# A new load order and a newly searched instruction list for a pre-LN block with memory attention and a SiLU feed-forward

## The chip, the cores and the metric

The kernel runs on one core of a Trainium2 chip. The time is the device time of one execution, in microseconds (us). A core has five engines that run their own instruction streams and meet only at semaphores: TensorE (PE in the profile, its weight loads PEld), VectorE (DVE), ScalarE (ACT), GpSimd (POOL) and SyncE (SP). SP does nothing here but issue transfers; ACT issues some as well.

## The reference

x is 2048 tokens by 640, in bf16.

```python
h  = x + A(layernorm(x), wq, wk, wv, wo, beta)
h2 = h + silu(layernorm(h) @ w1) @ w2            # w1 640 x 1728, w2 1728 x 640
# A: 32 heads of 20, the tokens in 4 segments of 512, for each segment s:
a_dot = softmax(q k^T * scale + causal mask) @ v     # inside the segment
a_mem = (phi(q) @ M) / (phi(q) @ z + 1e-6)           # phi(t) = t + 1 if t > 0 else exp(t)
o     = g * a_mem + (1 - g) * a_dot                  # g = sigmoid(beta), per head
M    += phi(k)^T @ v ;  z += sum(phi(k))             # for the segments behind
# A returns o @ wo
```

## The kernel before, in words

Everything stays in the core's memories; each weight is loaded once. The tokens are worked on in blocks of 128 (16 blocks, four to a segment). For a block the layer norm is three tasks: `n1_st` (two BN_STATS and a BN_AGGR on DVE, lines 728 and 731), `n1_r` (the reciprocal root on POOL, lines 741 and 744, its first step on DVE line 738 where the list says so) and `n1_ap` (DVE, line 750, writes `xn_rot`). The first four blocks are transposed on PE against an identity (`n1_tp`, line 759) and copied to `hT` by ACT (`n1_te`, line 768); later blocks are transposed by a transfer that SP issues (`n1_tr`, line 774, into `xT`).

wq and wk come in raw (into memory that `sT` uses later) and are rearranged into `wqr` and `wkr`, so that the heads lie on 32-row strips: ten tasks `re_wq0` to `re_wk4`, of two or three copies each, on DVE (line 694) or ACT (line 692). Then PE forms q and k in five chunks c for each of the two weights w (`pr`, line 837; in segment 0 each in two halves x and y of 256 tokens, so 5 matmuls of 256 columns per task), and ACT (line 845) or DVE (line 846) copies them out (`qe`). In segment 0 q and k lie in memory that w2 takes later, so the profile calls them `w_sb`; from segment 1 on they are `QK`. Twelve small copies by DMA per segment (`vt`, line 877) put together the last three groups of heads; they are issued by SP or ACT. `v` (line 802) and its copies `ve` (ACT line 812, DVE line 813) give the values `Vx`.

The heads are worked on in eight groups g of four. Scores are `qk` on PE (line 914), the exponential `e` on ACT (line 925, into `PT`, two heads at a time), the causal mask `mk` on POOL (line 936), probabilities times values `av` on PE (line 957), its copy `oe` (ACT line 970, DVE line 972), `tn` and `nm` (lines 986, 990 and 1003 to 1031) transpose back, add the memory term and divide. phi is `ex` on ACT (line 852) and `pha`, `phb` on DVE (lines 859 and 865); the memory update is `kt` (a transposing transfer, line 1071), `mz`, `ma`, `mb` (line 1079 ff.). Then come the output projection (`ot`, a transposing transfer, line 1132, and `wo`, line 1140), the second layer norm (`n2_`), the feed-forward `h1` (line 1175; its last part line 1169), `th` and `s` (tanh on ACT line 1184, product on DVE line 1190), `h2` (line 1217), the sum `o` (DVE line 1230) and the store `out` (line 1235).

No planner runs when the kernel is built. The string ORDER lists all 1479 tasks; `Graph.schedule` (line 287) goes down the list, and each task adds its instructions at the end of its engine's stream. An entry is the task's name, after a slash the engine where the task may choose (A is ACT, D is DVE, G is POOL, S is SP; without it the first that the task allows), and behind the colon the numbers of the buffers that it takes. So the list sets, for every engine, the order of its instructions; the waits follow from which task reads or writes what. An engine that waits holds up all that is behind it in its stream. `fillN` stands for N matmuls of zeros (line 614), which nothing reads.

The first loads are issued by lines 576 and 579. Before the change SP issues x0 (block 0), wq, three fifths of wv, beta, x4 (blocks 4 to 7), wo and w1 with the last rows of w2; ACT issues x1, x2, x3, wk, the rest of wv and x8 (blocks 8 to 11). `warm` (line 595) is a tanh on ACT that brings in the table of functions.

## Time and profile before

| what | value |
|---|---|
| device time, three executions | 310.89, 307.36 and 311.02 us, median 310.89 |
| profiled execution: span from first to last instruction | 307.5 us |
| PE busy | 293.9 us, 96% of the span |
| ACT busy | 224.4 us, 73% |
| DVE busy | 221.8 us, 72% |
| POOL busy | 141.3 us, 46% |
| read from HBM, written | 10.41 MB, 2.62 MB |
| mean granted TensorE clock | 0.989 |

The profiled execution's own time is not listed apart from its span; the span of 307.5 us is close to the lowest of the three times. In the profile, the busy shares by slices show where an engine is full, the granted clock (PEclk) in tenths shows where TensorE ran below full speed, the timeline gives start and duration of merged runs of like instructions ("x10" is ten of them), and a note in square brackets gives the idle time ahead of a row and what ended it. The matmuls are pipelined, so a run of n of them takes less than n times the duration of one.

### The profile page before, as it was taken

How to read it: one execution, taken by the hardware profiler on the slowest of the kernel's cores; microseconds unless marked ns; L12 is line 12 of the kernel's file. 1: busy time of each engine (PE TensorE's matmuls, PEld its weight loads, DVE VectorE, ACT ScalarE, POOL GpSimd, SP SyncE). 2: the span in 40 equal slices, each digit the busy share in tenths (PEclk: the TensorE clock that was granted, in tenths of full speed). 3: DMA queues.
4: the chain of work that ended last, by engine and by line, in shares of the span. 5: the costliest groups of instructions: out<-in, count | busy, mean ns of one | idle time of the engine just before them, and what ended most of it. 6: DMA issues, size and time to landing. Idle time of an engine off the chain costs nothing.

```text
span 307.5 us, 7509 instructions
## 1 busy us (share of the span) xinstructions
PE 293.9 (96%) x3010; PEld 171.8 (56%) x3010; DVE 221.8 (72%) x513; ACT 224.4 (73%) x319; POOL 141.3 (46%) x271
## 2 busy tenths in 40 slices
PE   7699889999999999997999999999999999999996
PEld 5476545455555555655553554466664557764574
DVE  5679877879669498986689886857965686834533
ACT  3489998999999889996859899986679851004500
POOL 7569652424654746752655445663573530100000
PEclk9689999999999999999999999999999999999999
DMA  7993624405465310144153320224220004221001
GB/s 262 316 370 84 114 61 126 107 19 159 83 90 110 41 33 9 35 81 52 38 120 95 67 36 17 36 52 92 64 66 23 0 3 84 66 65 44 0 30 58
DMA packets 48738, 24.66 MB, mean 80 GB/s; under 512 B 39168, under 2 KB 47616, under 8 KB 48704
## 3 DMA queue, kind: packets, MB, share of 16 engines
q1 hardware_dynamic: 44884, 19.62, 28.4%
q10 hardware_dynamic: 3820, 4.56, 5.0%
q8 instruction: 24, 0.39, 0.5%
q14 instruction: 10, 0.08, 0.1%
HBM read 10.41 MB, written 2.62 MB: 42 GB/s over the span
## 4 chain that ended last, share of the span: by engine, by line
PE 74%; ACT 9%; DVE 7%; DMA 6%; issue 1%; ACTq 1%; SPq 1%; DVEq 0%
PE ps_all L1217 20%; PE ps_all L1175 15%; PE ps_all L837 11%; ACT PT L925 7%; PE ps_all L914 7%; PE ps_all L1140 6%; PE ps_all L957 5%; PE ps_all L802 5%; DMA sT<-in_A_wk_dram 3%; PE ps_all L986 2%; DMA oT<-otok 2%; PE ps_all L1079 1%; PE ps_all L990 1%; DMA w_sb<-w_sb 1%; DVE stt L728 1%; DVE oTs L972 1%
## 5 line engine op out<-in xcount | busy, mean ns | idle before, releaser
L925 ACT ACTIVATE PT<-ps_all 128x1024 bf16<-128x1024 f32 (+1 forms) x168 | 157.0, 986 | 14.4 <-PE ps_all L914 12.5
L936 POOL TENSOR_SCALAR_AFFINE_SELECT PT<-PT 128x512 bf16<-128x512 bf16 x128 | 82.6, 651 | 78.3 <-ACT PT L925 75.1
L1217 PE MATMUL ps_all<-w_sb,sT 128*128 128x320 bf16 (+2 forms) x462 | 65.1, 295 | 0.1
L1175 PE MATMUL ps_all<-hT,w_sb 128*128 128x512 bf16 (+1 forms) x325 | 63.2, 337 | 0.0
L1184 ACT ACTIVATE th<-ps_all 128x512 f32<-128x512 f32 (+2 forms) x70 | 34.6, 508 | 37.8 <-PE ps_all L1169 19.5
L1217 PEld LDWEIGHTS ps_all<-w_sb,sT 128*128 128x128 bf16 x462 | 43.6, 98 | 18.8 <-issue 1.8
L1190 DVE SCALAR_TENSOR_TENSOR sT<-th,ps_all 128x512 bf16<-128x512 f32 (+2 forms) x70 | 38.4, 562 | 20.0 <-ACT th L1184 19.4
L1175 PEld LDWEIGHTS ps_all<-hT,w_sb 128*128 128x128 bf16 x325 | 29.7, 98 | 24.4 <-issue 2.1
L728 DVE BATCH_NORM_STATS2 stt<-x_tok 128x6 f32<-128x320 bf16 x64 | 28.0, 479 | 2.8 <-DMA x_tok<-in_A_x_dram 2.4
L1230 DVE SCALAR_TENSOR_TENSOR x_tok<-ps_all,x_tok 128x640 bf16<-128x640 f32 (+3 forms) x18 | 13.3, 746 | 18.2 <-PE ps_all L1217 18.0
L1140 PE MATMUL ps_all<-wo_sb,oT 128*128 128x320 bf16 x160 | 24.4, 300 | 1.9 <-DMA oT<-otok 1.9
L1031 POOL TENSOR_TENSOR otok<-on 128x320 bf16<-128x320 bf16 x24 | 19.2, 800 | 15.2 <-DVE on L1023 15.2
L957 PE MATMUL ps_all<-PT,Vx 128*32 128x256 bf16 (+3 forms) x576 | 23.5, 287 | 1.2 <-DVE rd L1003 0.8
L744 POOL TENSOR_TENSOR rst<-rst,eps_c 128x1 f32<-128x1 f32 x32 | 18.5, 577 | 11.4 <-DVE rst L738 9.6
L846 DVE CAST QK<-ps_all 128x512 bf16<-128x512 f32 x25 | 17.2, 687 | 5.6 <-PE ps_all L837 5.3
L972 DVE TENSOR_SCALAR oTs<-ps_all,lsc 128x512 bf16<-128x512 f32 (+1 forms) x29 | 17.7, 617 | 4.8 <-PE ps_all L957 4.5
L1023 DVE TENSOR_TENSOR on<-ps_all,rd 128x640 bf16<-128x640 f32 x24 | 19.8, 824 | 0.8
L1140 PEld LDWEIGHTS ps_all<-wo_sb,oT 128*128 128x128 bf16 x160 | 14.7, 98 | 9.4 <-DMA oT<-otok 2.2
L750 DVE TENSOR_SCALAR xn_rot<-x_tok,mvt,rst 128x640 bf16<-128x640 bf16 x32 | 15.7, 498 | 5.2 <-POOL rst L744 5.2
L837 PE MATMUL ps_all<-xT,wqr 128*128 128x512 bf16 x75 | 18.7, 380 | 0.3 <-ACT PT L925 0.3
L837 PE MATMUL ps_all<-xT,wkr 128*128 128x512 bf16 x75 | 18.7, 380 | 0.1
L957 PEld LDWEIGHTS ps_all<-PT,Vx 128*32 128x32 bf16 x576 | 12.4, 96 | 10.8 <-issue 3.5
(82 smaller groups left out, 347.9 us busy)
## 6 DMA issues: line engine op xcount, KB each, us to landing
w_sb<-in_B_w_dram SPq DMA_DIRECT2D x5, 432.0 KB, 15.1
out_dram<-x_tok SPq DMA_DIRECT2D x11, 160.0 KB, 1.8
x_tok<-in_A_x_dram SPq DMA_DIRECT2D x2, 640.0 KB, 8.0
w_sb<-in_B_w_dram SPq DMA_DIRECT2D x2, 480.0 KB, 3.8
sT<-in_A_wq_dram SPq DMA_DIRECT2D x1, 800.0 KB, 5.3
sT<-in_A_wk_dram ACTq DMA_DIRECT2D x1, 800.0 KB, 10.7
wo_sb<-in_A_wo_dram SPq DMA_DIRECT2D x1, 800.0 KB, 15.6
QKV<-QK SPq DMA_DIRECT2D x10, 72.0 KB
```

The source lines that it names most:

```text
L728: T.add(DV, lambda e, hh=hh: e.bn_stats(out=stt[:, s, 6 * hh:6 * hh + 6], in_=xb[:, 320 * hh:320 * hh + 320]), reads=R((xa, xsub)), writes ...
L837: fns = [lambda e, kc=kc: e.matmul(bank(ps)[:, lo:hi], lhsT=wt[:, kc, c, :], rhs=xT_[:, kc, lo:hi], start=(kc == 0), stop=(kc == NC - 1)) ...
L914: fns.append(lambda e, j=j, o=o, r=r, q0=q0, q1=q1, qa=qa, ka=ka: e.matmul(ps_all[:, o:o + q1 - q0], lhsT=ka[32 * r:32 * r + DH, 128 * j:1 ...
L925: T.add(AC, lambda e: e.activation(out=pt[:, pta.slot, q0:q0 + 2, 0:width], in_=sc3[:, b0:b0 + 2, 0:width], func=ACT.Exp, scale=SCALE), re ...
L936: T.add(PO, lambda e: e.affine_select(out=v, in_=v, pattern=[[0, 4], [1, 128]], compare_op=ALU.is_ge, fill=0.0, base=0, channel_multiplier ...
L957: fns.append(lambda e, j=j, r=r, h=h, pa=pa, pt=pt, co=co, q0=q0, ji=ji: e.matmul(bank(po)[32 * r:32 * r + 32, q0:hi], lhsT=Vx[:, vx.slot, ...
L972: f = lambda e: e.tensor_scalar(out=o, in0=i_, scalar1=lsc[:, g:g + 1], scalar2=None, op0=ALU.mult)
L1140: fns.append(lambda e, c=c, hh=hh: e.matmul(bank(ps, hh)[:, 0:320], lhsT=oT[:, c, 128 * i:128 * i + 128], rhs=wo_sb[:, c, 320 * hh:320 * h ...
L1175: fns = [lambda e, c=c: e.matmul(bank(ps)[:, lo:hi], lhsT=w1_sb[:, c, 128 * f:128 * f + 128], rhs=hT[:, c, lo:hi], start=(c == 0), stop=(c ...
L1184: T.add(AC, lambda e: e.activation(out=th[:, tha.slot, lo:hi], in_=bank(ps)[:, lo:hi], func=ACT.Tanh, scale=0.5), reads=R((ps, [0])), writ ...
L1190: T.add(DV, lambda e: e.scalar_tensor_tensor(out=sT[:, f, lo:hi], in0=th[:, tha.slot, lo:hi], scalar=1.0, in1=bank(ps)[:, lo:hi], op0=ALU. ...
L1217: fns.append(lambda e, f=f, t0=t0, fr=fr, hh=hh, n=n: e.matmul(bank(pa, hh)[:, 0:n], lhsT=sT[:, f, t0:t0 + 128], rhs=w2_sb[:, fr, c0 + 320 ...
```

## The change

Two things change: the declared load tasks, and the whole list ORDER. The rest of the code is the same; the list has 1479 entries before and after. The profile's line numbers fall by 2 in front of the loads' calls and by 4 behind them.

```diff
@@ ORDER, all lines replaced; its first lines
-epsc:0 zpad mt0 iota vpad0 sel x1:3 n1_st1:6 mta0 mtb0 mm6 mm4 mt2 mm2 x0:7 x2:5 mta2 x3:4 mtb2 epsg0 mm7 mt1 mt3
...
+halfc:0 x0:0 iota zpad fill23:5 sel mt1 beta warm:0 epsc n1_st0:0 x1:1 n1_st1:1 x2:2,3 n1_r0 n1_ap0:0 n1_st2:2 n1_r1
...
@@ the first loads
     load_x(0, 1, -100, 2.30, "fix", (SP,))
     load_x(1, 1, -100, 2.33, "fix", (AC,))
-    load_x(2, 1, -97, 4.79, "fix", (AC,))
-    load_x(3, 1, -96, 4.82, "fix", (AC,))
     load_w("q", wraw[:, 0, :, :], cw(A_wq), -99, 6.58, [(sT0, ["q"])], "fix", (SP,))
-    load_w("k", wraw[:, 1, :, :], cw(A_wk), -99, 8.51, [(sT0, ["k"])], "fix", (AC,))
-    load_w("wv0", wv_sb[:, 0:3, :], cw(A_wv[0:384, :]), -95, 4.96, [(W["wv"], [0])], "fix", (SP,))
-    load_w("wv1", wv_sb[:, 3:5, :], cw(A_wv[384:640, :]), -95, 4.96, [(W["wv"], [1])], "fix", (AC,))
+    load_w("k", wraw[:, 1, :, :], cw(A_wk), -99, 8.51, [(sT0, ["k"])], "fix", (SP,))
+    load_x(2, 2, -97, 4.79, "fix", (SP,))
+    load_w("wv", wv_sb[:, :, :], cw(A_wv), -95, 4.96, [(W["wv"], [0, 1])], "fix", (SP,))
```

wk moves from ACT's queue to SP's; blocks 2 and 3 become one load on SP; wv becomes one load on SP; x8 moves to SP. The code declares wq and wk ahead of blocks 2 and 3, but the list issues blocks 2 and 3 first. The 37 fillers in one run become 23, 4 and 4. Counted over the lists, ACT has 9 instead of 15 copies `qe` of 256 columns, 8 instead of 5 of 512, 5 instead of 10 copies `ve`, 4 instead of 2 `oe` of 256 and 7 instead of 9 of 512; what ACT gives up DVE takes. Three of the ten rearrangements are on ACT instead of one. ACT issues 16 instead of 8 of the small copies `vt`.

The stream of SP, at its start, before the change (`w_sb` stands for w1, w2 and the memory that q and k share with w2; `in_B_w_dram` for w1 and w2 in HBM):

```order
L576 DMA x_tok<-in_A_x_dram 128x640
L579 DMA sT<-in_A_wq_dram 128x5x640
L579 DMA wv_sb<-in_A_wv_dram 128x3x640
L591 DMA beta_bc<-in_A_beta_dram 128x32
L576 DMA x_tok<-in_A_x_dram 128x4x640
L579 DMA wo_sb<-in_A_wo_dram 128x5x640
L579 DMA w_sb<-in_B_w_dram 64x640
L579 DMA w_sb<-in_B_w_dram 128x1728 x5
```

And the same place now:

```order
L574 DMA x_tok<-in_A_x_dram 128x640
L587 DMA beta_bc<-in_A_beta_dram 128x32
L574 DMA x_tok<-in_A_x_dram 128x2x640
L577 DMA sT<-in_A_wq_dram 128x5x640
L577 DMA sT<-in_A_wk_dram 128x5x640
L574 DMA x_tok<-in_A_x_dram 128x4x640
L577 DMA wo_sb<-in_A_wo_dram 128x5x640
L577 DMA wv_sb<-in_A_wv_dram 128x5x640
L574 DMA x_tok<-in_A_x_dram 128x4x640
```

The values' weights stand behind wk, blocks 4 to 7 and wo; the five loads of w1 have left the start and come later in SP's stream, between transposing transfers.

The stream of ACT, at its start, before the change:

```order
L576 DMA x_tok<-in_A_x_dram 128x640 x3
L579 DMA sT<-in_A_wk_dram 128x5x640
L579 DMA wv_sb<-in_A_wv_dram 128x2x640
L595 ACT_TABLE_LOAD
L595 ACTIVATE w_sb<-zpad 128x1280
L576 DMA x_tok<-in_A_x_dram 128x4x640
```

And now:

```order
L591 ACT_TABLE_LOAD
L591 ACTIVATE w_sb<-zpad 128x1280
L574 DMA x_tok<-in_A_x_dram 128x640
L764 ACTIVATE hT<-ps_all 128x5x128
L688 ACTIVATE wqr<-sT 128x5x4x20
L688 ACTIVATE wqr<-sT 128x5x4x12
```

The load of block 1 stands behind the table load and the warming tanh, and it is ACT's only one of the first loads.

The stream of PE up to the second scores of segment 0, before the change:

```order
L614 MATMUL ps_all<-zpad 128x256 x37
L759 MATMUL ps_all<-ident,xn_rot 128x128 x10
L837 MATMUL ps_all<-hT,wqr 128x256 x10
L759 MATMUL ps_all<-ident,xn_rot 128x128 x5
L837 MATMUL ps_all<-hT,wkr 128x256 x10
L759 MATMUL ps_all<-ident,xn_rot 128x128 x5
L837 MATMUL ps_all<-hT,wqr 128x256 x5
L914 MATMUL ps_all<-w_sb 128x256 x4
L914 MATMUL ps_all<-w_sb 128x128 x4
```

And now:

```order
L610 MATMUL ps_all<-zpad 128x256 x23
L755 MATMUL ps_all<-ident,xn_rot 128x128 x5
L610 MATMUL ps_all<-zpad 128x256 x4
L755 MATMUL ps_all<-ident,xn_rot 128x128 x5
L610 MATMUL ps_all<-zpad 128x256 x4
L755 MATMUL ps_all<-ident,xn_rot 128x128 x5
L833 MATMUL ps_all<-hT,wqr 128x256 x15
L833 MATMUL ps_all<-hT,wkr 128x256 x10
L755 MATMUL ps_all<-ident,xn_rot 128x128 x5
L910 MATMUL ps_all<-w_sb 128x256 x4
L910 MATMUL ps_all<-w_sb 128x128 x4
```

The same four transposes and five products stand ahead of the first scores; all three products with wq now come ahead of the two with wk, and fillers stand between the transposes.

200 lines of the change are left out of this document (99 added, 101 removed).

## The prediction

> **What bounds the kernel now.** I read the page first, its busy shares in 40 slices (7.7 us each) and its chain of waits.
>
> ```profile
> PE   7699889999999999997999999999999999999996
> ACT  3489998999999889996859899986679851004500
> PEclk9689999999999999999999999999999999999999
> PE 74%; ACT 9%; DVE 7%; DMA 6%; issue 1%; ACTq 1%; SPq 1%; DVEq 0%
> ```
>
> PE is full from the third slice on, ACT nearly full from there to about 140 us, and the clock is low in the second and third slices. So a new list can win at the start, and behind it only where PE or ACT idles or does less. The table by stage says how much that is (PE, PEld, DVE, ACT and POOL busy, then clock, DMA share, GB/s):
>
> ```profile
> 0.00:17.34 17.34, 12.41 (x82) 9.02 (x82) 10.14 (x42) 7.33 (x14) 10.73 (x49) 0.81 0.88 297
> 17.34:34.43 17.09, 16.19 (x189) 11.22 (x189) 15.10 (x45) 16.67 (x31) 14.31 (x34) 1.00 0.65 184
> 60.00:80.00 20.00, 19.71 (x247) 11.35 (x247) 16.39 (x43) 19.79 (x33) 8.11 (x13) 1.00 0.34 86
> 40.00:260.00 220.00, 215.30 (x2355) 119.93 (x2356) 169.65 (x373) 187.28 (x253) 110.67 (x180) 1.00 0.31 62
> ```
>
> At 17.34 us the first scores start. Ahead of them no engine is full; the transfers are (0.88 of their time). From 17.34 to 34.43, where the first heads put together by DMA begin, PE (16.19 of 17.09) and ACT (16.67) are both full, around 70 us too; from 40 to 260 us PE is idle for 4.7 us in all; at the end, by the slices, PE alone is full.
>
> PE's timeline at the start, merged:
>
> ```profile
> 1.11 5.51 PE L614 MATMUL ps_all<-zpad 128*128 128x256 bf16 x37 [1.11 <-DVE zpad L593]
> 7.75 0.81 PE L759 MATMUL ps_all<-ident,xn_rot 128*128 128x128 bf16 x10 [1.13 <-DVE xn_rot L750]
> 10.00 1.71 PE L837 MATMUL ps_all<-hT,wqr 128*128 128x256 bf16 x10 [1.44 <-DVE wqr L694]
> 13.50 2.32 PE L837 MATMUL ps_all<-hT,wkr 128*128 128x256 bf16 x10 [1.25 <-DVE wkr L694]
> 17.34 0.38 PE L914 MATMUL ps_all<-w_sb 20*128 20x256 bf16 x8
> 24.35 1.27 PE L837 MATMUL ps_all<-hT,wkr 128*128 128x256 bf16 x10
> 27.63 1.52 PE L802 MATMUL ps_all<-wv_sb,hT 128*128 128x320 bf16 x10
> ```
>
> Ten products take 1.27 us at full clock (24.35) and 2.32 at half (13.50). PE waits for the rearranged wq, then for wk. DVE and ACT show since when wk could be had:
>
> ```profile
> 3.81 0.89 DVE L728 BATCH_NORM_STATS2 stt<-x_tok 128x6 f32<-128x320 bf16 x2 [1.73 <-DMA x_tok<-in_A_x_dram]
> 4.73 0.21 DVE L731 BATCH_NORM_AGGREGATE mvt<-stt 128x2 f32<-128x12 f32 x1
> 10.09 0.43 DVE L750 TENSOR_SCALAR xn_rot<-x_tok,mvt,rst 128x640 bf16<-128x640 bf16 x1
> 13.02 0.74 DVE L694 COPY wkr<-sT 128x400 bf16<-128x400 bf16 x4 [2.50 <-DMA sT<-in_A_wk_dram]
> 5.30 0.57 POOL L744 TENSOR_TENSOR rst<-rst,eps_c 128x1 f32<-128x1 f32 x1
> 13.02 0.83 ACT L692 ACTIVATE wkr<-sT 128x400 bf16<-128x400 bf16 x2 [3.48 <-DMA sT<-in_A_wk_dram]
> ```
>
> wk is there at 13.02, and both engines stood idle for it.
>
> **The change, part one: the loads.** These rows give the order of size, the time to landing, and what all queues moved:
>
> ```profile
> sT<-in_A_wq_dram SPq DMA_DIRECT2D x1, 800.0 KB, 5.3
> sT<-in_A_wk_dram ACTq DMA_DIRECT2D x1, 800.0 KB, 10.7
> x_tok<-in_A_x_dram SPq DMA_DIRECT2D x1, 160.0 KB, 2.8
> x_tok<-in_A_x_dram ACTq DMA_DIRECT2D x1, 640.0 KB, 15.4
> 0.00:8.00 8.00, 5.76 (x42) 4.43 (x42) 4.72 (x13) 2.55 (x2) 5.70 (x29) 1.00 0.79 267
> 7.00:8.00 1.00, 0.24 (x5) 0.25 (x5) 0.97 (x4) 0.00 (x0) 0.54 (x3) 1.00 1.08 381
> 20.00:21.00 1.00, 1.00 (x12) 0.89 (x11) 0.97 (x4) 1.00 (x2) 0.29 (x3) 1.00 1.05 408
> ```
>
> By 8.00 us 267 GB/s times 8 us = 2.14 MB had moved, but wk shared the way with wv, x4 and wo and landed at 13.0. Now SP's queue holds x0, beta, x2 with x3, wq, wk in this order, and ACT's x1: 160 + 8 + 320 + 800 + 800 + 160 = 2248 KB, or 2.30 MB, up to the end of wk. At the same pace that is 0.16 MB after 8.00 us; at 381 GB/s, 8.4 us, with some 0.3 us until the waiting engine sees it about 8.8 us: 4.2 us earlier. wq ends 819 KB (2.2 us) ahead of it, at 6.6 us, as it did before (issued at 1.25, 5.3 to landing). One queue alone can hold this pace: ACT's last load, x8, landed 15.4 us after its issue at 3.53, at 18.9, so at 20 us only SP's loads of w1 were on the way, with 408 GB/s. What is pushed back has room: x4, wo, wv and x8 are 2880 KB behind wk, 7.8 us, so wv is there at about 15 us and x8 at 17, and the first values' product stood at 27.6 us. Cost 0; were the cover gone, each us of lateness of wv would stop PE one us.
>
> x1 stands behind the warming tanh in ACT's stream. What that costs is seen before the change, where x8 stood behind both, too:
>
> ```profile
> 3.46 1.28 ACT L595 ACT_TABLE_LOAD   x1 [3.46 <-issue]
> 3.53 0.47 ACTq L576 DMA_DIRECT2D x_tok<-in_A_x_dram  x1
> ```
>
> Its issue began 0.07 us after the table load, so ACT's sequencer runs ahead of the engine. x1 is issued at about 1.1 us and lands at 4 to 5 us, when DVE is through with block 0 (4.86). Price 0; if the tanh did hold it (until 3.4 us), 1.4 us.
>
> **Part two: from the loads to the first scores.** I follow the new streams with the durations above. One block's statistics take 1.05 us on DVE (3.81 to 4.86), the root 0.93 after the aggregate (4.94 to 5.87), an apply 0.43, two copies of the rearrangement 0.4 (four 0.74, three some 0.5). DVE: block 0 to 4.86, block 1 to 5.95, apply 0 to 6.4, block 2 to 7.4, apply 1 to 7.8, wq chunk 0 to 8.2, apply 2 to 8.8 (its root is there at 8.3), wq chunk 1 to 9.1, block 3 to 10.3, wk chunks 0 and 2 to 11.0, wq chunk 4 to 11.45, apply 3 to 11.85, first copy of k to 12.2. ACT: `n1_te0` 6.8 to 7.5, wq chunk 2 to 8.3 (0.83, as at 13.02), `n1_te1` to 9.0. PE: transposes at 6.4, 7.8 and 8.8 with fillers between, three wq products (15 matmuls) 9.2 to 10.9, two wk products to 11.75, the last transpose to 12.25, first scores at 12.4. Against 17.34 that is 4.9 us earlier, with the clock full.
>
> The clock decides how much of it stays:
>
> ```profile
> 10.00:11.00 1.00, 1.00 (x8) 0.87 (x9) 0.52 (x3) 0.00 (x0) 1.00 (x4) 0.82 0.92 313
> 17.00:18.00 1.00, 1.00 (x14) 0.45 (x13) 1.00 (x6) 0.64 (x3) 1.00 (x7) 0.77 1.10 358
> ```
>
> A mean of 0.82 and one of 0.77 put the fall to half at 10.6 us and the return to full at 17.5, 6.8 us later. Ahead of the fall lay 3.4 us (6.62 to 10.00) with 0.81 us of matmuls in them, 24% busy; ahead of the return PE worked without a pause from 13.50. Now fillers end at 1.11 + 23 x 0.149 = 4.5 us, and from there to 9.2 us PE has three transposes of 0.4 and eight fillers, 2.4 of 4.7 us: 51% busy, between what lost the clock and what won it back. If it falls near 7 us and comes back after half of those 6.8, the second and third transposes, a filler run and some products take double, 1.5 us more, scores at 13.9; if it stays low for all 6.8 us, every product does, about 15.3. I take the middle of full clock and one half stretch, 13.1: **-4.2 us** at the first scores, with ends -4.9 and -2.0.
>
> The Trainium skill, "TensorE: Matmul & The Clock Gate", section "Part 1: The HAM clock gate (the "warmup" mystery)", says that the clock halves after at least one idle window of about 3.4 us and is full again after a busy one. The fall above came without such a gap (the longest had 1.44 us), while the 6.8 us do look like two such windows. By that rule the clock stays full here, since no gap is over 1.9 us, and the sum would be 0.7 us lower.
>
> **Part three: the first stage of scores.** From 17.34 to 34.43 us PE has 16.19 us of work, and the new list leaves it the same (15 products, 6 scores, 4 values in the same sequence), so this stage moves as a whole: 0. What ACT gives up is priced by its copies:
>
> ```profile
> L812 ACT ACTIVATE Vx<-ps_all 128x640 bf16<-128x640 f32 x10 | 7.1, 709 | 0.4 <-PE ps_all L802 0.4
> L970 ACT ACTIVATE oTs<-ps_all,lsc 128x512 bf16<-128x512 f32 x9 | 6.3, 697 | 3.8 <-PE ps_all L957 3.7
> L845 ACT ACTIVATE w_sb<-ps_all 128x256 bf16<-128x256 f32 x15 | 5.3, 389 | 1.1 <-PE ps_all L837 0.9
> L845 ACT ACTIVATE QK<-ps_all 128x512 bf16<-128x512 f32 x5 | 3.0, 603 | 0.6 <-PE ps_all L837 0.6
> ```
>
> Segment 0: six copies of 256 columns and one of values less, two `oe` of some 0.45 more, -2.1 us; PE is as full there, so I take 0 and keep -2.1 for the lower end. Segments 1 to 3: three copies of 512 columns more, four of values and two `oe` less, -2.4 us, where ACT is full in part of the time and PE in all of it: **-0.5**, ends 0 and -2.4.
>
> Against this ACT issues eight more of the small copies:
>
> ```profile
> L877 ACTq DMA_DIRECT2D QKV<-QK x5: 667/715/772, 83.0 to 200.8; - x5
> ```
>
> Eight times 0.715 is 5.7 us of its sequencer. As with x8 above, issuing goes on while ACT still executes; it costs only where the stream behind it has run dry. I take **+0.3**, ends 0 and 5.7.
>
> **Part four: the rest of the list.** PE's gaps from 40 to 260 us, 4.7 us by the stage table, are what another list could remove. The new list has the same stages behind 40 us, group for group, with a few products, masks and transfers in other places. I take 0; below, 4.7 could go, above, as much could come. The end (last product, sum, store of a 128-column piece) is as before: 0.
>
> **The sum.** -4.2 - 0.5 + 0.3 = -4.4 us on a span of 307.5, so 303.1 us for an execution like the profiled one. That execution is like the lowest of the three; the other two, and so the median, lie 3.4 us above. I know of nothing in the change that removes this difference, so the forecast for the median is 310.89 - 4.4 = **306.5 us**, 1.4% faster.
>
> **The rivals.** A measurement of this kernel tells about 2%, 6.2 us, from no change: faster means under 304.7, slower over 317.1.
>
> First, more is gained than the start: clock full (-4.9), and ACT's lighter load counts in segment 0 and behind it (-2.1 and half of -2.4). For it speaks ACT's 19.79 of 20 us, against it PE's 19.71 beside it. -8.2 us: 302.7.
>
> Second, the gain is given back before 35 us, because DVE becomes the bound of the first stage of scores. It has 15.10 us of work in 17.09; five more copies of 256 columns come to it in this stage (0.38 each, 1.9 us), and two rearrangements (0.5 each) that used to lie ahead: 18.0 us, 0.9 over. Its copies of q and k stand in line with the statistics of later blocks, so PE would wait for them. With the clock's bad end (-2.0) and this, -1.1: 309.8. Against it speaks that the statistics are for later segments and can be placed in gaps. The change's doing less than it says belongs here: if SP's one queue gave wk only the pace of before (13.0 us), all of part one would go, and the time would be some 310.9.
>
> Third, the slower side: w1.
>
> ```profile
> w_sb<-in_B_w_dram SPq DMA_DIRECT2D x5, 432.0 KB, 15.1
> 59.33 0.71 PE L1175 MATMUL ps_all<-hT,w_sb 128*128 128x256 bf16 x5
> SPq L774 <- DVE xn_rot L750: 12.7, 5, 6.3
> ```
>
> Before, its five loads were on the way from the start and PE never waited for one. Now the last of them stands in SP's stream behind four transposes of segment 1 and two of `oT`, each of which waits for DVE. The feed-forward's first product stood at 59.33 us on PE, now some 55; PE takes its stream in order, so all scores behind it would wait. The last w1 should be issued at about 40 us, with 432 KB on the way for 1.2 us and more. The longest wait of SP's queue for an applied block was 6.3 us; two of these in a row and the longest landing that a load of w1 took in the crowd of the start (15.1 us, median) make 40 + 12.6 + 15.1 = 67.7, 12.7 us late: 310.89 - 4.4 + 12.7 = 319.2. It decides from a landing behind 55 us. Against it: SP's stream is nearly empty from 40 to 60 us, and a load alone landed in 2.8.
>
> **How the numbers follow.** The forecast has 0.50, more gained 0.27, given back 0.16, w1 late 0.07. The forecast's own range is 303.5 to 309. For 8 in 10 I go down to **301**, below the first rival by half of the gaps that could go, and up to **311**, past the second and to no change. Faster by over 2%: most of the first rival and a fifth of the forecast, **0.34**; slower by over 2%: less than half of the third, **0.03**; within 2%: **0.63**.
>
> **What would show it.** Right: wk's first copy by 9 to 11 us on DVE, no wait for it on ACT; first scores between 12.4 and 14; half clock for at most 3.4 us; heads put together by DMA begin at about 30; the first feed-forward product near 55, without a wait for a transfer; gaps on PE behind 40 us of 3 to 6 us. The forecast is wrong if the first scores come after 15.5, if DVE is over 95% busy from 13 to 30 us with PE waiting for its copies, or if the difference at 60 us is not there at the end.

## The result, and the profile after

| kernel | median (lowest to highest) | runs | ratio to before, 95% interval |
|---|---|---|---|
| before | 309.10 us (307.36 to 311.36) | 20 | |
| the change | 307.67 us (306.48 to 311.53) | 20 | 0.9945 [0.9922, 0.9968] |

The change makes the kernel 0.55% faster, some 1.4 to 1.7 us. Ratios are formed from undisturbed runs alone, which leaves out those more than 1.5% above the fastest of their kernel. The profiled execution after took 307.58 us with a span of 305.8 us; device time is span plus 1.7 to 1.9 us in every run that lists both (1.8 there), so the profiled execution before (span 307.5) took about 309.3 us, near the median of its twenty runs.

From the page of the kernel after, PE, ACT, the clock and the chain of waits:

```profile
PE   7898899999999999999988999999999998999996
ACT  4999978998999989878798889887878750004500
PEclk9999979999999999999999999999999999999999
PE 66%; DVE 16%; DMA 7%; ACT 5%; POOL 2%; issue 2%; SPq 1%; ACTq 0%; DVEq 0%
```

The low clock has left the second and third slices and come back in the sixth. ACT is less full behind the first stage. The chain now runs over DVE for 16% of the span instead of 7%, and over PE for 66% instead of 74%.

The table by stage of the kernel after (columns as in the prediction):

```profile
0.00:12.92 12.92, 9.71 (x76) 7.22 (x77) 8.74 (x34) 7.84 (x18) 5.35 (x21) 1.00 0.85 276
12.92:29.76 16.84, 15.90 (x190) 11.17 (x189) 13.45 (x43) 15.76 (x28) 12.42 (x31) 1.00 0.52 138
60.00:80.00 20.00, 19.01 (x244) 11.62 (x234) 16.45 (x48) 18.71 (x30) 9.03 (x21) 1.00 0.56 137
40.00:260.00 220.00, 212.01 (x2295) 120.20 (x2312) 169.07 (x378) 182.32 (x246) 113.04 (x198) 1.00 0.32 65
```

The first scores start at 12.92 us, 4.42 us earlier, and the heads put together by DMA at 29.76, 4.67 earlier. But from 40 to 260 us PE is idle for 8.0 us where it had been idle for 4.7. The start has given what it should, and the rest has taken two thirds of it.

How much is left at each place is seen by starting times. Count the exponentials in their order on ACT (line 925 before, 921 after) and subtract, for the nth, the start before from the start after. The last column is the end of the last matmul. Heads stand in another order in the two lists, so a few tenths in the middle columns mean nothing.

| lead, us (kernel after minus kernel before) | 0th | 16th | 24th | 40th | 96th | 112th | 128th | 160th | end |
|---|---|---|---|---|---|---|---|---|---|
| the change | -4.0 | -4.7 | -3.0 | -3.0 | -2.8 | -4.2 | -3.4 | -2.9 | -1.5 |

The timeline of PE and the rows of DVE and ACT for wq and wk in the kernel after:

```profile
9.29 0.45 PE L755 MATMUL ps_all<-ident,xn_rot 128*128 128x128 bf16 x5 [1.14 <-DVE xn_rot L746]
9.81 1.81 PE L833 MATMUL ps_all<-hT,wqr 128*128 128x256 bf16 x15
11.46 1.25 PE L833 MATMUL ps_all<-hT,wkr 128*128 128x256 bf16 x10
12.92 0.34 PE L910 MATMUL ps_all<-w_sb 20*128 20x256 bf16 x8
...
8.33 0.55 DVE L690 COPY wqr<-sT 128x400 bf16<-128x400 bf16 x2 [1.13 <-DMA sT<-in_A_wq_dram]
10.69 0.73 DVE L690 COPY wkr<-sT 128x400 bf16<-128x400 bf16 x4
...
0.80 1.28 ACT L591 ACT_TABLE_LOAD   x1 [0.80 <-PEq L1274]
1.11 0.42 ACTq L574 DMA_DIRECT2D x_tok<-in_A_x_dram  x1
```

Nothing waits for wk any more (it landed at 10.6 us, 0.1 us before DVE turned to it), PE works at full clock from 9.81 to 38.7 us, and x1 is issued 0.31 us behind the start of the table load, not behind its end. But DVE and ACT now wait for wq.

### The profile page after: what moved, and what is told of

Read it like the earlier page. It is cut to its first block, busy times and chain, and to the rows that moved or that the text cites. A ratio compares the mean times of both kernels' runs of the same rounds, so it can differ in the third digit from the quotient of the medians.

```text
span 305.8 us, 7481 instructions
## 1 busy us (share of the span) xinstructions
PE 289.6 (95%) x2983; PEld 171.0 (56%) x3004; DVE 221.1 (72%) x518; ACT 223.3 (73%) x316; POOL 140.1 (46%) x269
## 4 chain that ended last, share of the span: by engine, by line
PE 66%; DVE 16%; DMA 7%; ACT 5%; POOL 2%; issue 2%; SPq 1%; ACTq 0%; DVEq 0%
PE ps_all L1213 17%; PE ps_all L833 12%; PE ps_all L1171 12%; PE ps_all L910 7%; PE ps_all L1136 6%; PE ps_all L798 5%; PE ps_all L953 4%; ACT PT L921 3%; DVE stt L724 3%; DMA sT<-in_A_wq_dram 2%; DMA x_tok<-in_A_x_dram 2%; PE ps_all L982 2%; DVE xn_rot L746 2%; DVE on L1019 1%; DVE Vx L809 1%
## 5 line engine op out<-in xcount | busy, mean ns | idle before, releaser
L1171 PE MATMUL ps_all<-hT,w_sb 128*128 128x512 bf16 (+1 forms) x316 | 61.5, 336 | 3.0 <-ACT PT L921 0.8
L746 DVE TENSOR_SCALAR xn_rot<-x_tok,mvt,rst 128x640 bf16<-128x640 bf16 x32 | 17.4, 553 | 3.2 <-POOL rst L740 3.2
L1144 DVE TENSOR_TENSOR x_tok<-ps_all,x_tok 128x640 bf16<-128x640 f32 x16 | 13.1, 821 | 8.9 <-PE ps_all L1136 8.7
L798 PE MATMUL ps_all<-wv_sb,xT 128*128 128x320 bf16 x120 | 19.4, 313 | 0.0
L833 PE MATMUL ps_all<-xT,wqr 128*128 128x512 bf16 x68 | 17.3, 380 | 1.4 <-issue 0.5
```

The costliest lines, as they stand in the source:

```text
L746: T.add(eng, lambda e: e.tensor_scalar(out=xn_rot[:, xn.slot, :], in0=x_tok[:, b % 12, :], scalar1=mvt[:, s, 0:1], scalar2=rst[:, s, :], o ...
L798: fns.append(lambda e, c=c, hh=hh: e.matmul(bank(ps, hh)[:, 0:320], lhsT=xT_[:, c, 128 * i:128 * i + 128], rhs=wv_sb[:, c, 320 * hh:320 * ...
L833: fns = [lambda e, kc=kc: e.matmul(bank(ps)[:, lo:hi], lhsT=wt[:, kc, c, :], rhs=xT_[:, kc, lo:hi], start=(kc == 0), stop=(kc == NC - 1)) ...
L1171: fns = [lambda e, c=c: e.matmul(bank(ps)[:, lo:hi], lhsT=w1_sb[:, c, 128 * f:128 * f + 128], rhs=hT[:, c, lo:hi], start=(c == 0), stop=(c ...
```

## The experiments

Each kernel was timed against the kernel before on the same chip, with 6 to 12 executions of its own. Six of them use the list of before (three of these with the start of the change's list) and six that of the change, so that loads and list can be told apart. "Full clock" means a mean granted clock of 0.999 or more over the whole execution.

### The old list with the new loads

```diff
 ORDER of before, loads declared as in the change
-x0:7 x2:5 mta2 x3:4 mtb2 ... w_k:0 w_wv1:0 ... w_q ... w_wv0 beta x4:0,1,2,6 ... w_wo:0 ... x8/A:8,9,10,11
+x0:7 beta x2:5,4 w_q:0 w_k mta2 mtb2 ... x4:0,1,2,6 ... w_wo:0 w_wv:0 x8:8,9,10,11
```

> The list of before (37 fillers in one run, same order on PE, DVE, POOL), but its first loads issued as in the changed kernel: SP x0, beta, x2 with x3, wq, wk, x4, wo, wv, x8, and x1 on ACT. Theory (the loads alone bring the start forward, the rest of the new list gives part of it back): first copy of wk on DVE at 10 to 11 us instead of 13.0, first scores at 13 to 15 us instead of 17.34, and the end 2.5 to 4 us earlier than before, so earlier than the changed kernel. Rival (the start is won by the new order on PE and the fillers): first scores at 16 us or later, the end within 0.8 us of before.

Measured: 307.27 us (305.79 to 308.43), ratio 0.9946 [0.9922, 0.9970]. The loads alone give as much as the whole change. The lead is 2.72 us at the first exponential, 2.70 from there to the 96th, and 3.44 from the 112th to the end: what is gained at the start is still there at the end, to a few hundredths. So nothing in the middle of this kernel absorbs a lead by itself. (The step behind the 96th is PE's wait for `oT` near 138 us, 1.90 us before and 1.18 here.) Not all of this lead is the loads': the profiled execution of before had half the clock from 10.64 to 17.47 us, this one had full clock throughout. Among executions at full clock the two kernels differ by 1.7 us (medians 308.06 of fourteen and 306.32 of five).

### The new list with the old loads

```diff
 ORDER of the change, loads declared as before
-halfc:0 x0:0 ... beta ... x1:1 ... x2:2,3 ... w_q:0 w_k ... w_wo:0 ... w_wv:0 ... x8:8,9,10,11
+halfc:0 x0:0 x1:1 w_q:0 x2:2 x3:3 w_k w_wv0:0 w_wv1 beta x4:4,5,6,7 w_wo:0 ... x8/A:8,9,10,11
```

> The changed kernel's list, but its first loads issued as before: SP x0, wq, three fifths of wv, beta, x4, wo; ACT x1, x2, x3, wk, the rest of wv and, behind the tanh, x8. Theory: wk is again the last to come, so PE, which now asks for two products with wk ahead of the first scores, has them at 15 us or later, and the end is not earlier than before (309 to 311 us). Rival (the list makes the gain): first scores before 14.5 us and the end as in the changed kernel.

Measured: 310.10 us (308.30 to 311.99), ratio 1.0048 [1.0019, 1.0078]. The new list by itself makes the kernel slower. Its lead is 1.88 us at the first exponential, 1.6 at the 96th and 0.3 at the end of its profile.

### The new start, with the old rest behind it

The list of before with the new loads, but from the first instruction to the last transpose of block 3 in the order of the change (fillers 23, 4 and 4, three rearrangements on ACT, the first scores ahead of the second k chunk).

```diff
 ORDER of the kernel "old list, new loads"
-epsc:0 zpad mt0 iota ... fill37:0 ... n1_tp1:1 n1_te1/A:0 n1_tp0:6 ... zf0 re_wk4/D ... qk0x0:4 ...
+halfc:0 x0:7 iota zpad fill23:5 sel beta ... n1_tp0:0 fill4:5 ... n1_tp3:2 w_wo:0 qe020x:0 qk0x0:4 pr011x:1 ... zf0 ...
```

> The list of before with the new loads, and with the changed list's order from the first instruction to the last transpose of block 3 and the first scores put ahead of it (fillers 23, 4 and 4, three rearrangements on ACT, first scores ahead of the second k chunk); behind that the order of before. It tells the new start from the new rest. Theory A (the start is worth some 4 us, and the order of before hands it on whole, as it handed on the 2.7 us of the loads alone; it is the new rest that loses): first exponential 3.7 to 4.2 us ahead of before, the same lead from the 24th exponential to the end give or take the 0.7 us of the wait for oT, the time 304.8 to 306.2, 1.2 us or more under both the changed kernel and the list of before with new loads. Rival B (a lead over some 3 us is absorbed in the stage of the first scores, where PE, ACT and DVE are all near full, whatever the list): lead 3 us or less from the 24th exponential on, the time 306.5 to 307.5. Half clock at 7 to 12 us, if it comes, would show as a first exponential under 3 us ahead.

Measured: 307.13 us (305.96 to 308.47), ratio 0.9926 [0.9896, 0.9955]. Not the 304.8 to 306.2 of theory A. Eight of the twelve executions, the profiled one among them, did not have full clock (it was lost at the start, below; the other four have a median of 306.09), so the lead is better read from the next kernel, which has the same start and kept it: 3.61 us at the first exponential, 1.98 at the 16th. Rival B was right here: 1.6 us go inside the stage of the first scores.

### And two transposes issued earlier

In the list of before, `ot4` and `ot5` (the transposes of `oT` for blocks 4 and 5, line 1132) stand on SP behind two small copies, `vt210` and `vt24`. The copies wait for DVE.

```diff
-ot6:0 ... ot7 ... vt210/S e16e0:5 e16e2 vt24/S mb13:0 pha230:0 ot4 mk16e_0 mk16e_256 ot5
+ot6:0 ... ot7 ... ot4 ot5 vt210/S e16e0:5 e16e2 vt24/S mb13:0 pha230:0 mk16e_0 mk16e_256
```

> The kernel with the new start and the order of before behind it, and one more move: the two transposes of oT for blocks 4 and 5 stand on SP right behind those of blocks 6 and 7, ahead of two small copies for the next segment, which wait for DVE. Before, PE waited 1.90 us for them at 141 us, 1.18 us in the kernel with the old list and the new loads, 0 to 1.8 us in those with the new list. If it is their late issue: no wait of PE for oT near 138 us, 1.2 us or more under the same kernel without the move, 303.5 to 305. If it is the landing that the queue delays, or the copies put behind them make the next segment's heads late instead: the wait stays or moves to the scores of segment 2 (line 912), and the time is the same within 0.5 us.

Measured: 305.64 us (305.19 to 306.49), ratio 0.9877 [0.9839, 0.9916], 0.6 us over the range expected; the lead steps from 1.99 us at the 96th exponential to 3.98 at the 112th and stays. Against the profiled execution of before, in which PE waited 1.90 us for these transposes, the move is worth 2.0 us. Against the kernel of the section before it is worth less: PE waited 0.61 us there, and at full clock the medians are 306.09 us (four executions) and, with the move, 305.62 (five). Where 1.6 us of the start's lead went is seen in the timeline of PE and in the busy times from 20 to 34 us, of the kernel before (first row) and of this one:

```profile
20.98 0.34 PE L912 MATMUL ps_all<-w_sb 20*128 20x256 bf16 x8 [0.59 <-DVE w_sb L844]
31.55 0.35 PE L955 MATMUL ps_all<-PT,Vx 128*32 128x256 bf16 x8 [0.73 <-DVE Vx L811]
```

```profile
20.00:34.00 14.00, 13.53 (x155) 9.27 (x153) 12.11 (x34) 13.69 (x26) 12.29 (x24) 1.00 0.59 158
20.00:34.00 14.00, 11.45 (x136) 7.41 (x135) 13.73 (x38) 11.90 (x21) 11.92 (x22) 1.00 0.64 178
```

DVE is busy for 13.73 of 14.00 us, and PE, which was busy for 13.53 in the kernel before, has only 11.45 and waits for DVE's copies.

### The same move alone, on three kernels

The edit of the section before, first on the old list with the new loads:

```diff
-ot6:0 ... vt210/S e16e0:5 e16e2 vt24/S mb13:0 pha230:0 ot4 mk16e_0 mk16e_256 ot5
+ot6:0 ... ot4 ot5 vt210/S e16e0:5 e16e2 vt24/S mb13:0 pha230:0 mk16e_0 mk16e_256
```

> The list of before with the new loads, its own start, and the two transposes of oT for blocks 4 and 5 ahead of the two small copies on SP. The loads alone led by 2.70 us up to the 96th exponential, the move was worth 1.99 us in the kernel with the new start (lead 1.99 before it, 3.98 behind). If leads only add: 2.70 + 1.90 = 4.6 us by the profile, time 304.5 to 305, under the kernel with the new start and the same move (305.64), so that the new start, 0.9 us more ahead at the first exponential, is worth less than nothing, because DVE work that it puts off comes back at 20 to 32 us. If the new start is worth what it showed at the first exponential, this kernel is slower than 305.64.

Measured: 304.94 us (304.35 to 306.02), ratio 0.9861 [0.9819, 0.9902]. Its lead is 2.80 at the first exponential, 2.68 from the 16th to the 96th, 4.66 from the 112th to the end. The sum of the two leads came out to 0.1 us. And the kernel with 0.8 us less lead at the first scores ends 0.7 us further ahead (4.66 us against 3.97 at the end of two profiles that both have full clock). The medians, 304.94 and 305.64, say the same, but the intervals of the two ratios overlap.

Then the same two lines of diff on the kernel before, loads and all else untouched:

> The kernel before with nothing changed but the place of the two transposes of oT. If the 1.90 us that PE waited at 141 us come from their issue behind two copies that wait for DVE, the wait is gone and the time is 1.5 to 2 us under before, 307.0 to 307.5. If the wait only comes in some executions, the median moves less, 308 to 308.7. If the loads of the start have a part in it, the wait stays.

Measured: 306.95 us (306.00 to 308.65), ratio 0.9925 [0.9897, 0.9952]. Two instructions moved on SP, nothing else, and the kernel before gains at least as much as by the whole change (0.9925 against 0.9945; the intervals overlap). In the leads the move is a step of 1.98 us, from 0.35 at the 96th exponential to 2.33 at the 112th. The rows of PE and of SP's queue, before the move and with it:

```profile
134.41 1.33 SPq L877 DMA_DIRECT2D QKV<-QK  x2
135.78 3.58 SPq L1132 DMA_TRANSPOSE oT<-otok  x2
...
141.06 1.53 PE L1140 MATMUL ps_all<-wo_sb,oT 128*128 128x320 bf16 x10 [1.90 <-DMA oT<-otok]
```

```profile
130.19 5.22 SPq L1132 DMA_TRANSPOSE oT<-otok  x4
135.45 1.78 SPq L877 DMA_DIRECT2D QKV<-QK  x2
...
138.74 1.53 PE L1140 MATMUL ps_all<-wo_sb,oT 128*128 128x320 bf16 x10
```

The bracket is gone. The wait had stood in the profile of before as PE's longest single one; it is part of the 4.7 us of gaps from 40 to 260 us. It had two causes. The two transposes were issued late, the first at 135.78 us; and this one took 5.2 us to land, at 141.02, where each of the two ahead of it took 2.6. With 2.6 us it would have been there at 138.4, before PE came to its products at 139.16. Moved, the first is issued at 132.79 and lands at 135.47.

The same move in the changed list:

```diff
-ot6:0 ot7 vt210 mk16e_0 ... kt23:1 ... out1 rs6 ot4 phb141 ... mb12:0 ot5 wo7:2
+ot6:0 ot7 ot4 ot5 vt210 mk16e_0 ... kt23:1 ... out1 rs6 phb141 ... mb12:0 wo7:2
```

> The changed kernel with the two transposes of oT for blocks 4 and 5 moved up on SP, ahead of one small copy, one transpose of phiK and one store. In the profile of the changed kernel PE did not wait for them, in three other kernels with its list it waited 1.6 to 1.8 us at 138 us. If that wait comes and goes from run to run with the landing: the fastest runs stay at 306.5, the slower ones come down, median 306.7 to 307.2. If the spread of this list is the clock's: median as before, 307.5 to 307.9.

Measured: 308.44 us (307.37 to 310.84), ratio 0.9974 [0.9942, 1.0006]. No gain, and the fastest runs are not faster than the change's. In the changed list the wait is not always there: none in the profiled execution of the change, but in this kernel's relatives below it is. The two profiles that show it:

```profile
139.27 1.53 PE L1136 MATMUL ps_all<-wo_sb,oT 128*128 128x320 bf16 x10 [1.84 <-DMA oT<-otok]
```

```profile
138.23 1.53 PE L1136 MATMUL ps_all<-wo_sb,oT 128*128 128x320 bf16 x10 [1.64 <-DMA oT<-otok]
```

The first is the kernel with beta late, the second that with the end edited. In the second, SP issued the two transposes at 133.84 us, 0.10 later than in the change, whose row at this place, at 136.41, has no wait: it is the landing that differs from run to run, 2.6 us behind the issue in the change (136.31) and 4.3 in the other (138.18). The traces show what goes with it: in the second an instruction load of 16 KB, in the DMA queue that the profile names instruction, is under way from 135.84 to 136.97 us, between issue and landing; in the change the load of that size comes at 137.41, behind the landing. In six of the fourteen profiled executions here the first of these two transposes took 3.9 to 5.2 us, and in all six an instruction load (of 16 KB in five, of 8 KB in one) begins within 2.6 us of its issue; in the other eight it took 2.6 to 2.8 us, and no load of 16 KB begins in that time. No run tests this by an edit. Why the move does not bring the median down in this list stays open; the clock does not explain it, for at full clock the medians are 307.74 us (five executions) and 307.22 for the change (eleven).

### The end of the changed list

```diff
-ot15:0 wo15:5 ... h2_8_1 h2_9_1 ... n2_ap13:1 n2_tr13:0 o8 n2_tr14 ... n2_tr12 n2_tr15
+ot15:0 h2_9_1 wo15:5 ... h2_8_1 ... n2_ap13:1 o8 n2_tr12:0 n2_tr14 ... n2_tr15 n2_tr13
```

> The changed kernel with two edits near its end: six products of h2 moved ahead of the first output projection of segment 3, and of the last four transposes the one that is ready last is issued last instead of first. Theory (the two waits of PE for transposes, 0.82 and 0.49 us, are lost time, since PE is full from there on): both vanish and the end is 1.0 to 1.4 us earlier. Rival (the time is lost at the stores or in the products' spacing): less than 0.3 us.

Measured: 307.81 us (306.16 to 309.09), ratio 0.9970 [0.9950, 0.9990], not below the change, where 1.0 to 1.4 us were expected. The two waits that it is aimed at are gone in its profile, and from the 160th exponential to the end it loses 0.9 us where the change loses 1.4; but 1.64 us more were lost at 138 us in that execution. By these two profiles the end of the changed list costs about half a microsecond, not the whole loss; the medians do not show even that.

### The masks of POOL

```diff
-zpad fill23:5 sel mt1 beta ... mt2 ... mta2 ... mt0 mt3 ... mtb2 mta0 mm7 mta1 mm10 mtb1 mtb0 mta3 mm6 mm5 mm4 mm0 mtb3 mm3 ...
+zpad fill23:5 sel mt1 ... mt0 mta0 mtb0 mm6 mm4 mta1 mtb1 mt2 mt3 n1_st0:0 ... n1_r2 mm0 mm2 mm9 mm1 ... n1_r3/D mm3 mm5 ...
```

> The changed kernel, with the constants that POOL builds for the memory mask (25 small instructions, lines 649 to 659) moved from the stage of the first scores back into POOL's idle time at the start, as the list of before had it; nothing else. Theory A (the changed list loses part of its lead because POOL's causal masks stand in line behind these constants, PE waits for a mask at 28.87 and 37.32 us, is only 79 to 93% busy from 25 to 38 us, and then gets half the clock from 38.7 to 42.2 us): the two waits for POOL vanish (0.8 us), and if the waits are what costs the clock, the half-clock stretch too (1.4 to 1.7 us); mean clock 1.0, the time 0.8 to 2 us under the changed kernel's, 305.5 to 307. Rival B (the lead is taken by what comes after, the waits for DVE's copies at 29.76 and 35.57 us would only grow): the time stays at 307.5 to 308 and the lead by exponentials is again 3.0 us from the 24th on.

(The entries moved are 23.) Measured: 307.88 us (307.24 to 311.44), ratio 1.0000 [0.9960, 1.0039]. Neither the waits nor the median did what theory A said. The rows that end PE's gaps in this kernel:

```profile
29.17 0.35 PE L953 MATMUL ps_all<-PT,Vx 128*32 128x256 bf16 x8 [0.53 <-DVE Vx L809]
37.67 0.35 PE L953 MATMUL ps_all<-PT,Vx 128*32 128x256 bf16 x8 [0.47 <-POOL PT L932]
42.42 1.53 PE L798 MATMUL ps_all<-wv_sb,xT 128*128 128x320 bf16 x10 [1.27 <-DMA xT<-xn_rot]
```

One of the two waits for POOL is replaced by one for DVE at the same matmul, the other is still there, and where the change lost 1.7 us to a slow clock this kernel, at full clock, loses 0.9 us between the 24th and the 40th exponential, the 1.27 us wait for a transposed block in it. That block's transpose was issued at 34.91 us right behind three loads of w1, 432 KB each; the last of these landed at 41.90 and the transpose at 42.38, 7.5 us behind its issue, where the median of this profile's 59 transposes is 2.65. The executions of this kernel with a mean clock of 1.0 took 307.36 us on average (four), those of the change 307.33 (eleven). The medians show no cost of POOL's constants.

### Beta, and the fillers

```diff
-zpad fill23:5 sel mt1 beta warm:0 ... w_q:0 w_k re_wq0:0
+zpad fill23:5 sel mt1 warm:0 ... w_q:0 w_k beta re_wq0:0
```

> The changed kernel with one entry moved: beta's load (128 rows of 64 bytes) behind wk instead of behind x0. Theory (the 64-byte rows slow all 16 engines from 3 to 4 us, where only 75 GB/s moved): wq is seen by DVE and ACT at 7.3 to 7.7 us instead of 8.33, first scores 0.3 to 0.8 us earlier, the end 0 to 0.8 us earlier. Rival (the hole is the start of the queues, whatever stands there): wq within 0.2 us of 8.33 and no difference at the end.

Measured: 308.85 us (306.54 to 311.87), ratio 0.9981 [0.9949, 1.0014]. The queues' pace from 3 to 4 us, of the change and of this kernel:

```profile
3.00:4.00 1.00, 1.00 (x7) 0.73 (x5) 0.88 (x2) 0.36 (x1) 0.00 (x0) 1.00 0.71 75
```

```profile
3.00:4.00 1.00, 1.00 (x7) 0.74 (x5) 0.86 (x2) 0.36 (x1) 0.00 (x0) 1.00 0.99 350
```

The hole in the pace was beta's, and it is gone. But wq, which SP issued at 1.73 us instead of 2.20, was seen by DVE at 8.51 instead of 8.33, and the first exponential came 0.4 us later. The hole did not set when wq landed.

```diff
-n1_tp0:0 fill4:5 n1_ap1:1 ... n1_tp1:2 fill4:5 n1_te0:0
+n1_tp0:0 n1_ap1:1 ... n1_tp1:2 n1_te0:0
```

> The changed kernel without the two runs of four fillers between the first three transposes; the run of 23 stays. What the fillers are for is the clock: with them PE is 15 to 100% busy by microsecond from 5 to 10 us and the clock stays full. If the eight fillers (1.2 us of PE) keep it: the clock falls to half between 7 and 12 us for 3.4 us or more, first exponential 1.5 to 3 us later than the changed kernel's, time 309 to 310.5. If the run of 23 up to 5.5 us is enough, or the clock is not governed by what PE did there: first exponential and time as in the changed kernel within 0.3 us. If PE stood busy with fillers when an applied block was there, it would even be up to 0.3 us earlier.

Measured: 311.21 us (307.82 to 313.78), ratio 1.0021 [0.9982, 1.0060]. The first exponential came as late as expected, the median 0.7 us later. None of the twelve executions had full clock (the means are 0.984 to 0.994), which 11 of the change's 20 had. The windows around the fall, in this kernel:

```profile
4.89:8.30 3.41, 1.64 (x17) 0.95 (x14) 2.16 (x7) 0.70 (x1) 2.30 (x7) 1.00 1.05 356
8.30:15.12 6.82, 5.67 (x30) 4.17 (x31) 4.59 (x21) 4.75 (x14) 1.84 (x7) 0.50 1.07 365
```

Without the eight fillers the clock is half for 6.8 us, and the first exponential is 2.5 us later than in the change. The fillers do their work, though not always: the changed list with `ot4` moved (first pair) and the kernel with the new start and the old rest (second) have them, and these executions lost the clock all the same.

```profile
7.42:10.84 3.42, 1.54 (x18) 1.21 (x19) 2.62 (x10) 1.96 (x5) 1.56 (x5) 1.00 1.07 373
10.84:14.25 3.41, 3.41 (x19) 2.35 (x17) 2.22 (x12) 2.78 (x10) 1.25 (x4) 0.50 1.07 363
```

```profile
6.83:10.25 3.42, 1.46 (x15) 0.87 (x14) 2.37 (x8) 1.60 (x4) 1.82 (x7) 1.00 1.06 376
10.25:13.66 3.41, 3.41 (x19) 2.35 (x18) 3.34 (x14) 2.87 (x9) 2.69 (x10) 0.50 1.07 362
```

### The best of both

The kernel with the new start, the old rest and the move of `ot4` and `ot5`; what hangs on beta and one block's statistics are moved ahead of the first exponentials.

```diff
-n1_te2 re_wq4 n1_ap3:3 ... re_wk3 qe010x:0 n1_tp3:2 w_wo:0 ... zf0 re_wk4/D zf1 lsc0 lsc1 ... n1_st7:4
+n1_te2 re_wq4 zf0 n1_ap3:3 ... re_wk3 n1_st7:4 lsc0 qe010x:0 n1_tp3:2 lsc1 w_wo:0 ... re_wk4/D zf1 ...
```

> The kernel with the new start, the old rest and the move of oT, and in addition what hangs on beta (two small ACT instructions, a mask on POOL, a reduction on DVE) and one block's statistics moved ahead of the first exponentials, as the changed list has them; DVE stood idle there from 13.77 to 14.54 and for 0.7 us more around 16 us, waiting for them. If DVE is what takes 1.6 us of the lead back between the first exponential and the 16th (3.61 to 1.98 us): about 1 us of it stays, lead 2.8 to 3.2 us from the 16th on, waits of PE for DVE's copies at 21 and 27 us under half of 0.59 and 0.29, time 304.6 to 305. If ACT or PE is full there anyway: lead 2 us and 305.6 as in the kernel without.

Measured: 304.12 us (303.87 to 307.45), ratio 0.9857 [0.9804, 0.9910], 1.4% under before, the lowest median here and 0.5 us below the range expected; by the ratios it cannot be told from the old list with the new loads and the same move (0.9861). The lead is 3.44 us at the first exponential, 3.15 from the 16th on and 5.12 behind 140 us; 1.2 of the 1.6 us that DVE had taken back are kept.

## Why the prediction was right and where it was wrong

The time of 307.67 us lies 1.2 us above the forecast and within its range, and the likeliest case, within 2%, is what came. But two errors stand against each other in that number, and that they nearly cancel is luck: the gain was 1.4 us, not 4.4, and the median of before was 309.1, not the 310.89 of three runs. **The step that the profiled execution "is like the lowest of the three"** was wrong: by its own time of about 309.3 us it is like the median of twenty runs.

**Part one, the loads.** The mechanism held: DVE and ACT do not wait for wk, x1 is not held by the table load, and wv and x8 are waited for by nobody. The sizes were off. Two loads of the kernel after with their time to landing, and what all queues had moved by 8 us:

```profile
sT<-in_A_wq_dram SPq DMA_DIRECT2D x1, 800.0 KB, 6.1
sT<-in_A_wk_dram SPq DMA_DIRECT2D x1, 800.0 KB, 7.9
```

```profile
0.00:8.00 8.00, 6.00 (x41) 4.21 (x41) 4.25 (x13) 3.25 (x3) 3.31 (x15) 1.00 0.71 221
```

Issued at 2.20 and 2.71 us, wq landed at 8.3 and wk at 10.6, against 6.6 and 8.8 in the prediction; their distance of 2.3 us was forecast as 2.2. **The step that failed is "at the same pace"**: 221 GB/s by 8 us instead of 267 are 0.37 MB less, some 1 us. The rest is the assumption that a load is there when all bytes ahead of it have gone by. In the kernel with beta late the six windows from 1 to 7 us show 19, 286, 350, 211, 334 and 335 GB/s, so that wq and the blocks ahead of it (1.47 MB) had gone by at about 6.8 us, and wq was seen by DVE at 8.51. The Trainium skill, "DMA: Bandwidth & Descriptors", section "Why a DMA increments its semaphore by 16 and not by 1", says that a load runs on up to 16 engines which finish independently, and that its semaphore counts all of them; no row here shows the engines one by one, but a landing 1.7 us behind the mean pace fits it.

**Part two, to the first scores.** The forecast of 13.1 us met 12.92, by two errors that offset: the clock stayed full, as at the range's lower end, and wq was late. PE's first two transposes (5.70 and 7.26 us) came half a microsecond and more ahead of the working with full clock, 6.4 and 7.8; the third (9.29) came half a microsecond behind its 8.8, because its apply stands on DVE behind the first copies of wq. The prediction had the fall of the clock before the change right, at 10.6 us, but counted PE's work from 6.62 to 10.00 us, 24%; in the 3.41 us that end at the fall PE was busy for 1.45, 43%, not far from the 51% that it reckoned for the change. The clock rule of the Trainium skill that the prediction weighed ("TensorE: Matmul & The Clock Gate", Part 1) gave the right side in this profile. It does not cover all of them: in the windows of 3.41 us ahead of a fall, shown above, PE was busy for 1.46, 1.54 and 1.64 us, without an idle window anywhere. Its statement that the window runs freely, whatever the kernel does, the runs do support: the same start kept the clock in the change and lost it in two kernels, and the spans of half clock are 3.41 or 6.83 us long.

**Part three, the stage of scores.** In the change this stage did move as a whole: it took 16.84 us where it had taken 17.09, and the lead was 4.42 us at its start and 4.67 at its end. DVE is not its bound there:

```profile
20.00:34.00 14.00, 12.95 (x162) 8.25 (x164) 10.45 (x30) 13.17 (x21) 11.75 (x28) 1.00 0.48 100
```

In the old rest behind the new start it did not move as a whole. There 1.6 us of the lead went to DVE (13.73 of 14.00 us busy; the kernel that puts some of the work back ahead keeps 1.2 of them), so there the second rival had the mechanism right. The first scores come earlier partly because other work is put behind them. In the change the lead is lost right behind the stage: 1.7 us between the 16th exponential (at 32.25 us) and the 24th (at 42.06). PE's two longest gaps from 25 to 38 us, and the windows around the half clock:

```profile
28.87 0.35 PE L953 MATMUL ps_all<-PT,Vx 128*32 128x256 bf16 x8 [0.60 <-POOL PT L932]
35.57 0.35 PE L953 MATMUL ps_all<-PT,Vx 128*32 128x256 bf16 x8 [0.64 <-DVE Vx L809]
```

```profile
28.51:31.92 3.41, 2.71 (x42) 1.70 (x46) 3.15 (x11) 3.12 (x6) 1.78 (x5) 1.00 0.45 96
35.33:38.74 3.41, 2.72 (x51) 1.31 (x52) 3.25 (x13) 3.08 (x5) 3.34 (x7) 1.00 1.14 333
38.74:42.16 3.42, 3.42 (x27) 1.54 (x29) 1.74 (x5) 2.24 (x4) 0.10 (x1) 0.50 0.35 68
```

At full clock another wait comes in its place (the kernel with POOL's constants early), so the clock alone does not decide. That wait is for the transpose behind the three loads of w1. In the change the same transpose, issued at 34.80 us, landed at 41.56, within the stretch of half clock, so it does not show as a wait. In the kernel before and in the old list with the new loads w1 is loaded long before, and the transposes of these four blocks landed 2.6 to 3.4 us behind their issue. That w1's new place costs some of the lead here is read from the traces; no run moves these loads alone. Why the clock fell behind windows in which PE was busy for 2.72 us, when it held behind one of 2.48 us in the kernel with the new list and the old loads, is not settled.

Neither -0.5 us for ACT's lighter load nor +0.3 for its eight more small copies can be seen: from the 24th exponential to the 96th the lead stays between 2.7 and 3.3 us. Unless something else offsets them, the two together are a few tenths of a microsecond.

**Part four, the rest of the list.** This is where most of the gain went, and **the step that failed is "I take 0"**. It stood with 4.7 us either way, and 3 to 6 us of gaps behind 40 us were expected; there were 8.0. Of the 4.67 us of lead at the heads put together by DMA, 1.5 are left at the end. The longest waits of PE behind 156 us, in the change, and all of them in the old list with the new loads and the move of `ot4`:

```profile
PE ps_all L1136 <- DMA oT<-otok: 0.8, 1, 0.8
PE ps_all L1171 <- DMA hT<-xn_rot: 0.7, 2, 0.5
PE ps_all L1171 <- DVE sT L1186: 0.6, 1, 0.6
```

```profile
PE ps_all L1173 <- issue: 1.0, 6, 0.2
PE ps_all L984 <- DVE x_tok L1228: 0.2, 1, 0.2
```

The changed list loses 2.7 us from the 112th exponential to the end, the old one nothing; only the half microsecond at the very end was tried by an edit. What the list had won, the 1.90 us wait at 141 us, is won by moving two instructions. So the balance of the change, by the leads of one profiled execution, is: 4.0 us at the first exponential, of which the kernel with the loads alone has 2.7; 0.7 more up to the 16th; 1.9 lost up to the 96th; 1.5 won at the wait of 141 us; 2.7 lost behind it. 1.5 us are left.

This balance holds the clock, too. In the profiled execution of before the products from 13.50 to 17.34 us ran at half clock; by 1.27 against 2.32 us for ten products they would have taken some 1.7 us less at full clock (an estimate). The prediction's 4.2 us were reckoned against this execution, but of the 84 executions of before that were timed with the experiments 27 had full clock, with a median of 308.1 us, and 22 a mean below 0.992, as the profiled one had, with a median of 310.7. Eleven of the change's 20 had full clock, with a median of 307.2. So at full clock the change is worth about 0.9 us, and the rest of its 1.4 would be that it keeps the clock more often (an estimate, since these executions were not timed together).

The prediction's own sign of error was "if the difference at 60 us is not there at the end": it was 3.0 us at the 40th exponential and 1.5 at the end. The first rival (302.7) did not come: the clock was full, but nothing of ACT's lighter load showed. The third, w1, did not come as described: the first feed-forward product stood at 56.47 us with no wait ahead of it, and the loads of w1 took 4.0 us to land (median). What it does in its new place is the long landing of the transpose in part three.

## What to carry to other kernels

A lead at a milestone counts only together with the work that has been put behind it: before counting an earlier first product as gain, add up what the engine that feeds it (here DVE, 13.73 of 14.00 us) still has to do. The old list handed on a lead to some hundredths of a microsecond between waits, so two edits could be judged apart and added; a whole new order must be judged by its waits to the end, not by its start. And look first for the single long wait in the profile: one of 1.90 us, mended by issuing two transposes ahead of two copies that wait, was worth at least as much as the new loads and the new list together. Last, compare leads only between executions with the same clock: here one stretch of half clock at the start can stand in the lead as if an edit had won it.

## What the runs showed of the hardware

Beta's load, 8 KB in rows of 64 bytes to 128 partitions, cut the pace of all queues from some 300 to 75 GB/s for one microsecond where SP issued it second; moved behind wk, the pace there was 350. It is not the load alone that does it: behind wk its packets were on the way from 8.3 to 12.2 us, and the queues moved 297 GB/s or more in each of these microseconds.

PE's clock at the start fell to half behind windows of 3.41 us in which PE was busy for 1.46, 1.54 and 1.64 us, and held behind 1.60 and 2.21 us (in the kernel before it fell behind 1.45, in the new list with the old loads it held behind 1.67). So if busy time decides, the border at the start lies near 1.6 us, 47% of a window, and not sharply, since 1.60 held and 1.64 fell; at 38.74 us it fell behind 2.72, so busy time alone is not the rule. The windows that held, in the kernel after and in the last kernel of the experiments:

```profile
8.03:11.44 3.41, 2.21 (x22) 1.76 (x21) 3.04 (x14) 3.11 (x9) 1.17 (x5) 1.00 1.07 366
```

```profile
6.30:9.71 3.41, 1.60 (x18) 0.99 (x15) 2.20 (x8) 1.50 (x4) 2.06 (x7) 1.00 1.05 366
9.71:13.12 3.41, 3.18 (x30) 2.74 (x31) 3.33 (x16) 3.41 (x12) 1.78 (x6) 1.00 1.07 366
```

The same start gets one or the other, by where the windows lie in that execution: the kernel with the new start, the old rest and the move kept the clock with windows of 2.04 and 2.22 us, at 4.16 and 7.57 us, but in its stretch from 6.83 to 10.25 us, where the kernel without the move had a window and lost the clock, PE was busy for 1.54.

And the landing of a transposing transfer can differ by 1.8 us (2.6 and 4.3 us behind the issue) between two executions that issue it at the same time to 0.1 us; the long landings of this transfer went with an instruction load on the queues.
